# Gate stage of a fused attention and gated-MLP kernel: engine queues in the order of a walked list, row scales prepared a block further ahead, half of w_out decoded beside attention

## The chip, the cores and the metric

One core of one Trainium2 chip. The metric is device time in microseconds of one launch, median of several runs. Engines are named as in the profile: PE (TensorE matmul), PEld (its weight loads), DVE (VectorE), ACT (ScalarE), POOL (GpSimd), SP (SyncE, which issues all DMAs here).

## What is computed

```python
def phi(x):                                   # x: (8, 8, 576, 64), w_phi: (64, 128)
    proj = np.einsum('bhsd,df->bhsf', x, w_phi)
    proj = proj - np.max(np.abs(proj), axis=-1, keepdims=True)
    return np.concatenate([np.exp(proj), np.exp(-proj)], axis=-1)
q_p, k_p = phi(q), phi(k)
kv = np.einsum('bhsf,bhsd->bhfd', k_p, v); z = np.sum(k_p, axis=2)
num = np.einsum('bhsf,bhfd->bhsd', q_p, kv)
den = np.einsum('bhsf,bhf->bhs', q_p, z)[..., None] + 1e-06
x = (num / den).transpose(0, 2, 1, 3).reshape(4608, 512)
xn = x / np.sqrt(np.mean(x * x, axis=-1, keepdims=True) + 1e-06) * rms_g
g, val = xn @ w_gate, xn @ w_val              # (512, 1536) each
out = (g / (1 + np.exp(-g)) * val) @ w_out    # w_out: (1536, 512)
```

w_gate, w_val and w_out come as 64-bit floats, the rest as 32-bit.

## The kernel before

Every float32 product is made of three products of operands split into a high and a low half: ACT casts the high half (`_split`, L60) and DVE or POOL subtracts it to get the low one (L61). The 64-bit weights are first decoded to 32 bits by `_decode` (L41 to L56): two ACT scalings (L48, L49), three DVE bit operations (L50 to L52), two POOL multiplications of half the columns (L54) and a DVE addition (L55). The work runs in four stages, whose matmuls follow each other on PE.

**Attention** (loop at L497): 35 rounds over 32 head pairs. Each round merges four streams by place (`_merge`): transposes and projections of one pair, exponentials and the key-value sums of the pair before, the numerators of the one before that, and the division of the oldest, which writes x to DRAM. In each round one piece of `decode_jobs` (w_gate and w_val, 32 pieces) is decoded, placed by `late()` behind the engines' latest instructions. As blocks of 288 rows of x are done, `fill` (L453) multiplies them by the first three column groups of w_gate and w_val: 6 units of 12 matmuls a block (L467), ACT copies out (L470), and the result goes to DRAM unscaled ("raw columns").

**Drain** (L653): the fill units that are left are issued, and between them, `at_once` pieces each, the preparation of the first six weight sets (`prep_w`) and of block 0 (`prep`).

**Gate stage** (L849): 9 blocks of 512 rows, each with the 9 remaining column groups of the two weight matrices. One unit is one block and one column group; it makes the gate and value columns by a seven-product scheme (`Unit.p`), each product six matmuls (L680) in one of the PSUM banks A, B, E, two of each. PE's order is written by hand, with an issue edge from each product to the one before: 1, 5, 7', 2, 6, 3', 4', where a prime is the unit before. Between products ACT copies A to B (L697) and E to c (L702), makes the Silu of A (L706), copies B to u (L710); DVE adds B to c (L713), E to u (L716), multiplies h by B (L719); `end`, a unit later, makes Silu of u (L722, ACT), h's second half (L723, POOL) and stores h. Which instruction of DVE, ACT and POOL stands where is not written: the framework's scheduler sorts them by its own simulated times.

Beside the products run jobs hung on places in the loop (`job`, four places to a unit): `prep` of the next block (squares L591 and L594, POOL sums L595, two matmuls with ones L609 and L610 for the row sums, square root L611, reciprocals L615, normalisation L619, differences L630 and L633, seven operand splits); `gv_raw`, which scales and multiplies the raw columns (DVE L737, ACT L738, POOL L739); three more weight sets in block 0 (differences L544, splits L547 to L550); in blocks 1 to 6, 24 pieces of w_out decoded (L795) and written to DRAM; and in the last block the six operand sets of w_out, read back (L747, L757). A block's seven operands lie in nine buffers `xo`, so five of the next block's wait for the last unit's products.

**Output stage** (L943): 18 groups of 256 rows of h, loaded in one DMA each (`hload`), seven products with w_out (L959), and the output rows stored.

Of the kernel before, what the change touches and what calls it, by code (L numbers as in the profile page):

```python
# [10 lines left out]
I32 = mybir.dt.int32  # L11
# [29 lines left out]
def _decode(nc, pool, raw, n):  # L41
# [6 lines left out]
    nc.scalar.mul(a, high.bitcast(F32), REBASE)  # L48
    nc.scalar.mul(lf, low.bitcast(U32), 2.0 ** -52)  # L49
    nc.vector.tensor_scalar(p, u, 3, None, ALU.logical_shift_left)  # L50
    nc.vector.scalar_tensor_tensor(p, u, -0x80000000, p, ALU.bitwise_and, ALU.bitwise_or)
    nc.vector.tensor_scalar(u, p, -0x00800000, None, ALU.bitwise_and)  # L52
    for h in (slice(0, n // 2), slice(n // 2, n)):
        nc.gpsimd.tensor_tensor(a[:, h], lf[:, h], a[:, h], ALU.mult)  # L54
    nc.vector.tensor_tensor(a, p.bitcast(F32), a, ALU.add)  # L55
    return a  # L56
# [26 lines left out]
def kernel(ctx: ExitStack, tc: tile.TileContext, q, k, v, w_phi,  # L83
# [20 lines left out]
    XPAD, OPAD, RPAD = 192, 64, 192  # L104

# [53 lines left out]
    ps_f = ctx.enter_context(tc.tile_pool(name="ps_f", bufs=2, space=PSUM))  # L159
# [20 lines left out]
    a_ctx = ExitStack()  # L180
    dec = a_ctx.enter_context(tc.tile_pool(name="a_dec", bufs=1))
    ld = a_ctx.enter_context(tc.tile_pool(name="a_ld", bufs=2))
    wk = a_ctx.enter_context(tc.tile_pool(name="a_wk", bufs=2))
    const = a_ctx.enter_context(tc.tile_pool(name="a_const", bufs=1))
    pad(a_ctx, 192)
    big = a_ctx.enter_context(tc.tile_pool(name="a_big", bufs=2))
# [35 lines left out]
    def decode_jobs():  # L222
        jobs, late_ = [], []
# [16 lines left out]
        for j in range(NJ):  # L240
            for c0 in range(0, DM, CH):
                keep(late_, w_out, wos, j * 128, c0, CH)
        return jobs, late_

    def decode_pieces(jobs, dec):
        raws = {}

        def piece(i):
# [5 lines left out]
            with late():  # L254
                jobs[i][2](_decode(nc, dec, raw, jobs[i][1]))
# [219 lines left out]
    early, decs_late = decode_jobs()  # L475
# [21 lines left out]
    for i in range(PR + 3):  # L497
# [9 lines left out]
        dq += 1  # L507
# [16 lines left out]
        if PR - 2 <= i < PR:  # L524
            raw_gv(i - PR + 2)
    a_ctx.close()


    g_ctx = ExitStack()
# [8 lines left out]
    pg_ctx = ExitStack()  # L538
    ps_g = pool(pg_ctx, "m_ps_g", 2, space=PSUM)
    bank = lambda n: ps_g.tile([128, 512], F32, name=n)  # L540

    def sums7(w, rows):

        sub = lambda o, a, b, op=ALU.subtract: nc.vector.tensor_tensor(w[:, o], w[:, a], w[:, b], op)  # L544
        w_ = w.rearrange("p o c f -> p o (c f)")
        wt = rows.rearrange("p h o c f -> p h o (c f)")
        return sub, [lambda: nc.scalar.copy(wt[:, 0, 0:3], w_[:, 0:3]),  # L547
                     lambda: nc.gpsimd.tensor_tensor(wt[:, 1, 0:3], w_[:, 0:3], wt[:, 0, 0:3].bitcast(F32), ALU.subtract),
                     lambda: nc.scalar.copy(wt[:, 0, 3:7], w_[:, 1:5]),
                     lambda: nc.vector.tensor_tensor(wt[:, 1, 3:7], w_[:, 1:5], wt[:, 0, 3:7].bitcast(F32), ALU.subtract)]  # L550

    W = {}
    ROW = {1: 0, 2: 1, 4: 2, 3: 3, 6: 4, 5: 5, 7: 6}

    def prep_w(j, pl):

        d = {}

        def one_():
            d["w"] = w = raws.pop(j)  # L560
            W[j] = pl.tile([128, 2, 7, 2, 128], F32R, name=f"w{j}")
            d["sub"], d["p"] = sums7(w, W[j])
            d["sub"](4, 0, 3)
            d["sub"](3, 3, 2, ALU.add)
            d["p"][0]()
            d["p"][1]()

        def two():
            d["sub"](2, 3, 0)
            d["sub"](1, 1, 2)  # L570
            d["p"][2]()
            d["p"][3]()
        return [one_, two]

    def fetch(bk):
        x = xm.tile([128, NC, T], F32, name="x")
        nc.sync.dma_start(out=x, in_=xsv[:, :, bk * T:(bk + 1) * T])
        return x

    xb = {}  # L580
    seeds = []

    def prep(bk):

        d = {}
        ops = xb[bk] = {}

        def square(c):
            if c == 0:
                ops["ri"] = xm.tile([128, T], F32, name="ri", bufs=2)  # L590
                nc.scalar.activation(ops["ri"], d["x"][:, 0], AF.Square)  # L591
                return
            sq = xm.tile([128, T], F32, name="t", bufs=2)
            nc.scalar.activation(sq, d["x"][:, c], AF.Square)  # L594
            nc.gpsimd.tensor_tensor(ops["ri"], ops["ri"], sq, ALU.add)  # L595

        def total():
            sh = xm.tile([128, T], F32R, name="t", bufs=2)
            sl = xm.tile([128, T], F32R, name="t", bufs=2)
            _split(nc, sh, sl, ops["ri"], lo_eng=nc.gpsimd)  # L600
            d["s"] = sh, sl

        def scale():
            if not seeds:
                for _ in range(2):
                    seeds.append(bank("B"))
                    nc.tensor.matmul(seeds[-1], ones, d["s"][0], start=True, stop=True)
            sp = fp()
            nc.tensor.matmul(sp, ones, d["s"][0], start=True, stop=False)  # L609
            nc.tensor.matmul(sp, ones, d["s"][1], start=False, stop=True)  # L610
            nc.scalar.activation(ops["ri"], sp, AF.Sqrt, scale=1.0 / DM, bias=eps)  # L611

        def inverse(c):
            ri = ops["ri"][:, c * 256:(c + 1) * 256]
            nc.vector.reciprocal(ri, ri)  # L615

        def normal(c):
            x = d["x"]
            nc.vector.scalar_tensor_tensor(x[:, c], x[:, c], g[:, c:c + 1], ops["ri"], ALU.mult, ALU.mult)  # L619

        part = lambda k, h: d["x"][:, 2 * k:2 * k + 2, h * HT:(h + 1) * HT]

        def split(n, v, lo):
            o = xp.tile([128, 2, 2, HT], F32R, name="xo")
            _split(nc, o[:, 0], o[:, 1], v, lo_eng=lo)
            ops[n] = o

        def third():
            d["t3"] = xm.tile([128, 2, HT], F32, name="t", bufs=2)
            nc.vector.tensor_tensor(d["t3"], part(1, 1), part(0, 1), ALU.subtract)  # L630

        def sub(o, a, b):
            nc.vector.tensor_tensor(part(*o), part(*a), part(*b), ALU.subtract)  # L633

        P, V = nc.gpsimd, nc.vector
        return ([lambda: d.update(x=fetch(bk))]
                + [lambda c=c: square(c) for c in range(NC)] + [total, scale]
                + [lambda c=c: inverse(c) for c in range(2)] + [lambda c=c: normal(c) for c in range(NC)]
                + [third, lambda: split(1, part(0, 0), P), lambda: sub((0, 1), (0, 1), (0, 0)),
                   lambda: split(5, part(0, 1), P)],  # L640
                [lambda: split(2, part(1, 0), P), lambda: sub((0, 0), (1, 1), (0, 1)),
                 lambda: split(6, part(0, 0), P), lambda: sub((1, 0), (1, 0), (0, 0)),
                 lambda: split(7, d["t3"], P), lambda: split(3, part(1, 1), P), lambda: split(4, part(1, 0), P)])

    first, rest = prep(0)
    ahead = []
    for j in range(JL):
        ahead += prep_w(j, wl6) + [lambda j=j: raw_gv(j + 2)]
    pre = first + rest
    ahead = [ahead[0], pre[0]] + [p for ab in zip(ahead[1:], pre[1:]) for p in ab] + pre[len(ahead):]  # L650
    n = 0
    at_once = -(-len(ahead) // RES)
    while units or here or fills:  # L653
        if len(units) <= 6 and here:
            units.extend(fill(*here.pop(0), nc.gpsimd, [fp, lambda: bank("A")]))
        units.pop(0)()
        for _ in range(at_once):
            if ahead:
                ahead.pop(0)()
        load_x()  # L660
    while ahead:
        ahead.pop(0)()
    f_ctx.close()
    pad(ctx, RPAD, side="right")
    wr3 = pool(ctx, "w_r", 1, side="right")
    k_ctx = ExitStack()
    wk = pool(k_ctx, "wk", 2, side="right")

    def product(o, n, x, w, first):
        last = next(i for i in reversed(nc.cur_bb.bb.instructions) if i.engine == mybir.EngineType.PE)  # L670
        with tc.issue_after(last):
            product_(o, n, x, w, first)

    def product_(o, n, x, w, first):
# [10 lines left out]
    class Unit:  # L685
# [3 lines left out]
        def __init__(u, bk, j):  # L689
            u.bk, u.j, u.x, u.w = bk, j, xb[bk], W[j]  # L690

        def p(u, n):
            if n == 1:
                u.A = bank("A")[:, LO]
                product(u.A, 1, u.x, u.w, True)
                u.B = bank("B")[:, LO]
                nc.scalar.copy(u.B, u.A)  # L697
            elif n == 5:
                u.E = bank("E")[:, LO]
                product(u.E, 5, u.x, u.w, True)  # L700
                u.c22 = wk.tile([128, HT], F32, name="c22", bufs=3)
                nc.scalar.copy(u.c22, u.E)  # L702
            elif n == 2:
                product(u.A, 2, u.x, u.w, False)
# [318 lines left out]
```

## Time and profile before

| | us |
|---|---|
| median of 3 runs | 1378.99 |
| runs | 1374.15, 1385.33, 1378.99 |
| profiled execution, its own time | 1373.07 |
| span of that execution, first to last instruction | 1371.3 |
| granted TensorE clock, mean over the span | 0.972 of full speed |

A row of instructions reads: start, time on the engine, engine, source line, operation, tile written <- tiles read, shape, count; in brackets the idle time of that engine just before it and what ended it. A row of a group reads: line, engine, operation, tiles, shape, count, then busy us and mean ns of one, then idle time ahead of it and its causes. A row of a stage reads: from:to and its length, then for PE, PEld, DVE, ACT, POOL the busy us and the count of instructions, then the granted clock (1.00 is full speed), the share of the DMA engines' time in use, and GB/s. Matmuls overlap, so the distance of their starts is their price, not their own time; a few records of matmuls can be missing.

### The profile page before, as it was taken

The numbers are of one execution on the slowest core, as the hardware profiler recorded it, in microseconds if no ns is written. First come the engines' busy times: TensorE is split into PE (matmuls) and PEld (weight loads), VectorE is DVE, ScalarE is ACT, GpSimd is POOL, SyncE is SP. The second block draws the span as 40 slices with busy tenths as digits, with TensorE's granted clock in tenths as the row PEclk, the third lists the DMA queues.
The fourth block names the chain that finished last, engine by engine and source line by source line (L and its number), as shares of the span: only waits on it lengthen the run. The fifth ranks groups of instructions, "written<-read, shape, count | busy, mean of one in ns | idle before, by whom it ended". The sixth has DMA issues, their size and how long they took to land. (4 is left out here: it accounts for less than half of the span.)

```text
span 1371.3 us, 28126 instructions
## 1 busy us (share of the span) xinstructions
PE 1258.1 (92%) x10202; PEld 1233.9 (90%) x10202; DVE 1023.6 (75%) x1451; ACT 809.1 (59%) x1849; POOL 843.2 (61%) x775
## 2 busy tenths in 40 slices
PE   7989999999999986897988988889789889999998
PEld 7989999999999986896988988879789879999998
DVE  6898977888778746618477685776754769999996
ACT  5978876877787754444556555456455533343432
POOL 3665754566565565636556654665545457888885
PEclk9999999999999997999999999999999989999999
DMA  6456666566556336534443443434421443535441
GB/s 162 123 139 165 172 173 191 142 164 186 155 157 187 100 102 189 179 129 153 136 137 132 163 135 109 148 136 140 147 101 70 163 161 116 178 124 169 139 139 47
DMA packets 206698, 197.40 MB, mean 144 GB/s; under 512 B 69792, under 2 KB 173600, under 8 KB 206560
## 3 DMA queue, kind: packets, MB, share of 16 engines
q1 hardware_dynamic: 206560, 195.60, 46.5%
q8 instruction: 81, 1.33, 0.4%
q14 instruction: 57, 0.47, 0.1%
HBM read 126.04 MB, written 69.50 MB: 143 GB/s over the span
## 5 line engine op out<-in xcount | busy, mean ns | idle before, releaser
L373 POOL TENSOR_TENSOR ql<-eq,qh 128x256 fp32r<-128x256 f32 x256 | 216.4, 876 | 75.4 <-issue 51.8
L680 PE MATMUL B<-xo,w 128*128 128x256 f32 x1458 | 215.1, 285 | 5.7 <-DVE c L713 3.9
L680 PEld LDWEIGHTS B<-xo,w 128*128 128x128 f32 x1458 | 193.4, 196 | 7.2 <-DVE c L713 4.9
L680 PE MATMUL A<-xo,w 128*128 128x256 f32 x972 | 147.2, 289 | 36.7 <-ACT B L697 36.4
L680 PEld LDWEIGHTS A<-xo,w 128*128 128x128 f32 x972 | 129.4, 196 | 43.0 <-ACT B L697 42.3
L680 PE MATMUL E<-xo,w 128*128 128x256 f32 x972 | 144.0, 285 | 18.9 <-DVE u L716 18.8
L61 POOL TENSOR_TENSOR xo<-st,xo 128x768 fp32r<-128x768 f32 x54 | 126.8, 2360 | 44.7 <-ACT xo L60 42.9
L680 PEld LDWEIGHTS E<-xo,w 128*128 128x128 f32 x972 | 127.7, 194 | 22.8 <-DVE u L716 22.7
L308 DVE TENSOR_REDUCE mx<-pp 128x4 f32<-128x512 f32 (+1 forms) x160 | 101.0, 632 | 44.9 <-PE pp L306 43.4
L344 PE MATMUL acc<-vm,ek 128*128 128x65 f32 x1024 | 131.0, 267 | 0.7 <-ACT ek L331 0.5
L60 ACT CAST xo<-st 128x768 fp32r<-128x768 f32 x54 | 43.4, 836 | 148.9 <-DVE st L912 70.3
L723 POOL TENSOR_TENSOR h<-u,c 128x256 f32<-128x256 f32 x81 | 70.5, 870 | 96.8 <-ACT u L722 75.1
L344 PEld LDWEIGHTS acc<-vm,ek 128*128 128x128 f32 x1024 | 126.9, 192 | 1.2 <-ACT ek L331 1.2
L61 POOL TENSOR_TENSOR xo<-x,xo 128x512 fp32r<-128x512 f32 (+1 forms) x72 | 106.3, 1488 | 26.1 <-ACT xo L60 25.0
L467 PE MATMUL fp<-xo,fg 128*128 128x288 f32 x576 | 97.3, 308 | 8.1 <-ACT fo L470 6.6
L369 ACT ACTIVATE qh<-sm 128x512 fp32r<-128x512 f32 (+1 forms) x192 | 97.1, 506 | 0.0
L467 PEld LDWEIGHTS fp<-xo,fg 128*128 128x128 f32 x576 | 84.7, 196 | 9.8 <-ACT fo L470 7.7
L304 PE MATMUL pp<-wh,th 128*128 128x256 f32 x288 | 88.2, 307 | 4.6 <-DVE yr L311 3.4
L61 POOL TENSOR_TENSOR xo<-w,xo 128x768 fp32r<-128x768 f32 x36 | 91.6, 2543 | 0.0
L368 ACT ACTIVATE eq<-sm 128x512 f32<-128x512 f32 x128 | 78.3, 611 | 17.3 <-PE sm L357 16.5
L959 PE MATMUL gy<-w,xo 128*128 128x256 f32 x648 | 79.5, 281 | 6.2 <-ACT xo L60 5.6
L959 PEld LDWEIGHTS gy<-w,xo 128*128 128x128 f32 x648 | 76.9, 192 | 7.1 <-ACT xo L60 6.0
(164 smaller groups left out, 3439.3 us busy)
## 6 DMA issues: line engine op xcount, KB each, us to landing
w<-hs SPq DMA_DIRECT2D x18, 1536.0 KB
hs<-h SPq DMA_DIRECT2D x81, 256.0 KB
gvs<-fo SPq DMA_DIRECT2D x96, 144.0 KB
gvr<-gvs SPq DMA_DIRECT2D x54, 256.0 KB
rc<-di SPq DMA_DIRECT2D x32, 288.0 KB
x<-xs SPq DMA_DIRECT2D x16, 576.0 KB
x<-xs SPq DMA_DIRECT2D x9, 1024.0 KB
kt<-in_k_dram SPq DMA_DIRECT2D x32, 256.0 KB
```

The source lines that it names most:

```text
L60: (hi_copy or nc.scalar.copy)(hi, x)
L61: (lo_eng or nc.vector).tensor_tensor(lo, x, hi.bitcast(F32), ALU.subtract)
L304: nc.tensor.matmul(o, th[:, cs], wh, start=True, stop=False)
L308: nc.vector.tensor_reduce(mx[:, 0:2 * m], pp[:, 0:2 * m], axis=AX.X, op=ALU.max, apply_absolute_value=True)
L344: nc.tensor.matmul(acc[:, sg, h], e[h][:, sg, j], vm[:, h, j], start=False, stop=(h == 1 and j == T0 - 1))
L368: nc.scalar.activation(ei[:, sg], yi, AF.Exp, scale=1.0 - 2.0 * sg)
L369: nc.scalar.activation(hi[:, sg], yi, AF.Exp, scale=1.0 - 2.0 * sg)
L373: nc.gpsimd.tensor_tensor(lo[:, sg, cs], ei[:, sg, cs], hi[:, sg, cs].bitcast(F32), ALU.subtract)
L467: nc.tensor.matmul(fp[:, 0:TF], w, xx[x][:, c], start=(i == 0), stop=(i == 3 * NC - 1))
L680: nc.tensor.matmul(o, a, e, start=(first and i == 0), stop=(i == 5), skip_group_check=True)
L723: nc.gpsimd.tensor_tensor(u.h[:, HI], u.u2, u.c22, ALU.mult)
L959: nc.tensor.matmul(place[n], a[:, kp], w[:, o], start=(first and kp == 0 and i == 0), stop=(kp == KP - 1 and i == 2), skip_group_check=True)
```

## The change

- From the end of attention to the end of the gate stage, every instruction of DVE, ACT, POOL and PE gets an issue edge from the one before it on its engine (`InOrder`), so that each engine's queue is the order in which the program writes them. SP's DMAs get none.
- That order is made by `Flow`: a list of tasks with an engine (or two to choose from: PV, VP), a modelled duration, and what they depend on. The products are written one after the other; each advances a modelled time (0.685 us, 1.6 for a fill unit), its evictions are put at once on their engines (`core`), and then `step` writes those tasks of the list, by priority, whose inputs are modelled done and whose engine is free or will have finished within 1.2 us (1.9 in the drain). A task that a product needs and that is not yet written is written then (`need`). Loads are modelled at 5 to 7 us. The square root, 3 us with its tables, may go only behind product 1.
- The order of products is 1, 5, 7', 3', 2, 6, 4', the Silu of the second half follows product 6, u is kept in h's second half. B has three banks, A and E two, S one (row sums, and the difference for operand 5, which now goes to PSUM); the two fill banks end with the drain's first units, and later fill units use A and E.
- Row scales (`scales`) are a task set of their own, for the block after next, from four separate 256 KB loads of x; reciprocals are four of 128 columns for two of 256. `prep` loads x again.
- w_out: pieces 0 to 11 are decoded beside attention (1.6 pieces a round in rounds 12 to 31), with their last addition on POOL; 12 to 17 in the drain, in buffers of `xo`; the last six in blocks 1 to 6.
- Attention's pools are in another order in memory, constants and results lowest, decode buffers highest.

The diff's core:

```diff
-        dq += 1
+        dq += 1 + (ATT / 20 if 12 <= i < 32 else 0)
...
+                jobs[i][2](_decode(nc, dec, raw, jobs[i][1], nc.gpsimd if i >= 2 * NC + 24 else nc.vector))
...
+            def call(*a, **k):
+                with ExitStack() as es:
+                    if self.last is not None:
+                        es.enter_context(tc.issue_after(self.last))
+                    r = f(*a, **k)
+                self.last = next(i for i in reversed(tc.nc.cur_bb.bb.instructions) if i.engine == self.kind)
+                return r
...
+        def need(self, *ts):
+            for t in ts:
+                if t["done"] is None:
+                    self.run(t)
+                self.now = max(self.now, t["done"] + self.HOP)
...
+            if t["big"]:
+                return r <= self.now and self.free[e] <= self.now + 0.6 and self.roomy
+            return r <= (self.now if e in "QT" else max(self.now, self.free[e])) and (
+                e in "QT" or self.free[e] <= self.now + 0.05
+                or max(r, self.free[e]) + (t["dur"] if not isinstance(t["dur"], dict) else t["dur"][e]) <= self.now + self.room)
...
+            q.append(add("Q", 5.0, lambda c=c: chunk(c), a[c - 2] if c > 2 else scale_t[0], behind=q[-1:]))
+            s.append(add("S", 0.62, lambda c=c: square(c), q[c]))
+            a.append(add("P", 1.35, lambda c=c: total(c), s[0], s[c], a[c - 1]))
...
+        sc = add("T", 0.5, scale, l, after=("banks",), ring=ring["S"], frees=frees)
+        r = add("S", 3.0, root, sc, big=True)
+        inv = [add("V", 0.87, lambda c=c: inverse(c), r) for c in range(4)]
...
+        VP = dict(V=1.0, P=1.45)
+        f = add("Q", 7.0, fetch, *used[0])
+        nm = [add("V", 0.9, lambda c=c: normal(c), f, *inv) for c in range(NC)]
...
+            ld = ring["r"] = flow.add("Q", 6.0, load, behind=[ring["r"]], ring=ring["gvr"], frees=frees)
+            s = flow.add("V", 0.9, scaled, ld, *xt[bk]["ri"])
+            s = flow.add("S", 0.42, silu, s)
+            s = flow.add("PV", dict(P=0.95, V=0.5), mul, s)
...
     for bk in range(NB):
+        raw_block(bk)
         if bk + 1 < NB:
+            prep(bk + 1, JN - 1)
+        if bk + 2 < NB:
+            scales(bk + 2)
...
+        for j in order:
+            u = Unit(bk, j)
+            for who, n in ((u, 1), (u, 5), (old, 7), (old, 3), (u, 2), (u, 6), (old, 4)):
+                if who is None:
+                    continue
+                who.p(n)
+                if n == 6 and old:
+                    old.silu()
+                flow.roomy = n == 1
+                flow.step(1.2)
+            old = u
```

More of the change, by code (lines that the diff above doesn't have):

```diff
@@ L575, in fetch @@
[L575 to L586, printed above, removed]
-        def square(c):
[L589 to L601, printed above, removed]
+    BANKS = dict(A=2, B=3, E=2, S=1)
@@ L603, in scale @@
         def scale():
             if not seeds:
-                for _ in range(2):
+                for _ in range(BANKS["B"]):
                     seeds.append(bank("B"))
[L607 to L611, printed above, removed]
+                    nc.tensor.matmul(seeds[-1], ones, d["sh"], start=True, stop=True)
@@ L635, in prep @@
[L635 to L667, printed above, removed]
+        add = flow.add
+        q = [add("Q", 5.0, lambda: chunk(0), *scaled_t.get(bk - 3, ()))]
+        s = [add("S", 0.62, lambda: square(0), q[0])]
+        a = [None]
+        for c in range(1, NC):
+            q.append(add("Q", 5.0, lambda c=c: chunk(c), a[c - 2] if c > 2 else scale_t[0], behind=q[-1:]))
+            s.append(add("S", 0.62, lambda c=c: square(c), q[c]))
+            a.append(add("P", 1.35, lambda c=c: total(c), s[0], s[c], a[c - 1]))
@@ L669, in product @@
     def product(o, n, x, w, first):
[L670 to L674, printed above, removed]
         i = 0
@@ new lines, in fill_unit @@
+    def fill_unit(m, bk, j, wi, n):
+        d = xs_t[m]
+        flow.need(*d["t"])
+        js = slice(j * 128, (j + 1) * 128)
+        o = bank("AE"[n % 2])[:, 0:TF]
+        i = 0
+        for c in range(NC):
+            a, al = wf1[wi][:, 0, c, js], wf1[wi][:, 1, c, js]
+            for w, h in ((a, 0), (a, 1), (al, 0)):
+                nc.tensor.matmul(o, w, d["o"][:, h, c], start=(i == 0), stop=(i == 3 * NC - 1))
+                i += 1
+        flow.mark(("unit", n), 1.6)
+        f = fxp.tile([128, TF], F32, name="fo", bufs=6)
+        flow.core("S", 0.42, lambda: nc.scalar.copy(f, o))
+        nc.sync.dma_start(out=gvv[j][:, wi, bk * TF:(bk + 1) * TF], in_=f)
@@ new lines @@
+    flow.pri = -2
+    for m, (bk, x) in enumerate(blocks_left[:2]):
+        fill_tasks(m, bk, x)
+    flow.pri = -1
+    make_w(0, lambda: wl6, True)
+    scales(0)
+    for k in range(min(ATT, npieces), NDEC0):
+        decode_out(k, True)
+    prep(0)
+    make_w(1, lambda: wl6, True)
+    for j in range(2, JN):
+        flow.pri = -1 if j < JL else 0
+        make_w(j, lambda j=j: wl6 if j < JL else wr3, False, () if j < JL else ("right",))
+    flow.pri = 1
+    scales(1)
+    n = 0
+    while units:
+        units.pop(0)()
+        flow.mark(("unit", n), 1.6)
+        n += 1
+        if len(units) % (2 * J1) == 0:
+            flow.marks.add(("fill", len(units) // (2 * J1) and -2 or -1))
+        flow.step(1.9)
@@ new lines @@
+    pf_ctx.close()
+    pg_ctx = ExitStack()
+    ps_g = pool(pg_ctx, "m_ps_g", 1, space=PSUM)
+    flow.marks.add("banks")
+    for m, (bk, _) in enumerate(blocks_left):
+        for jj in range(2 * J1):
+            fill_unit(m, bk, *divmod(jj, 2), n)
+            n += 1
+            if jj == 0 and m + 2 < len(blocks_left):
+                flow.pri = -2
+                fill_tasks(m + 2, *blocks_left[m + 2])
+            if jj == 2 * J1 - 1:
+                flow.marks.add(("fill", m))
+            flow.step(1.9)
@@ L812 @@
+    f_ctx.close()
+    pad(ctx, RPAD, side="right")
+    wr3 = pool(ctx, "w_r", 1, side="right")
+    flow.marks.add("right")
+    k_ctx = ExitStack()
+    wk = pool(k_ctx, "wk", 2, side="right")
+    done = NDEC0
+    old = None
     for bk in range(NB):
-        for n in range(2 * J1):
-            job(bk, (n + 1) * NS, lambda bk=bk, n=n: gv_raw(bk, n))
-            job(bk, (n - 1) * NS, lambda bk=bk, n=n: load_r(bk, n))
+        order = LAST if bk == NB - 1 else range(JN)
+        flow.pri = 10 * bk + 3
+        raw_block(bk)
+        flow.pri = 10 * bk + 2
@@ L873 @@
-    older.end()
+            prep(bk + 1, JN - 1)
+        if bk + 2 < NB:
+            scales(bk + 2)
+        flow.pri = 10 * bk + 4
+        while done < NDEC0 + (npieces - NDEC0) * min(bk, NB - 3) // (NB - 3):
+            decode_out(done)
+            done += 1
+        if bk == NB - 1:
+            for kp in range(KP):
+                make_o(kp)
+            flow.add("Q", 7.0, lambda: hload(0), after=tuple((bk, LAST[HSLOT[0]], n) for n in ROW))
+        for j in order:
[9 more added lines that the diff above has]
+            old = u
```

538 lines of the change are left out of this document (347 added, 191 removed).

## The prediction, made before any run of the changed kernel

> **What bounds the kernel now.** I read the page first, then a table of busy time cut at the stages' ends, then who waited for whom on PE in the gate stage, then single instructions around one boundary of blocks.
>
> ```profile
> PE 1258.1 (92%) x10202; PEld 1233.9 (90%) x10202; DVE 1023.6 (75%) x1451; ACT 809.1 (59%) x1849; POOL 843.2 (61%) x775
> ```
>
> PE is the busiest engine, so the question is where it isn't working at full speed. By stage (us from:to, length, then busy us and count of PE, PEld, DVE, ACT, POOL, then granted clock and DMA share):
>
> ```profile
> 0.00:497.00 497.00, 474.54 (x3866) 466.12 (x3867) 400.67 (x712) 388.09 (x964) 289.59 (x372) 1.00 0.56 155
> 497.00:610.70 113.70, 95.70 (x653) 93.28 (x653) 50.76 (x45) 50.70 (x102) 58.34 (x38) 0.91 0.51 162
> 610.70:1097.80 487.10, 425.83 (x3420) 413.92 (x3418) 324.78 (x513) 269.51 (x641) 278.50 (x276) 0.96 0.40 134
> 1097.80:1122.90 25.10, 18.60 (x127) 17.68 (x128) 17.42 (x14) 7.29 (x11) 11.74 (x6) 0.80 0.46 151
> 1122.90:1371.30 248.40, 243.38 (x2144) 242.88 (x2142) 229.96 (x168) 93.49 (x134) 205.04 (x85) 0.99 0.40 132
> ```
>
> They are attention, the drain of the remaining fill units, the gate stage, the start of the output stage, and the output stage. What the middle two would take without loss comes from undisturbed neighbours, a fill unit of 12 matmuls and a gate product of 6:
>
> ```profile
> 588.30 1.76 PE L467 MATMUL fp<-xo,fg 128*128 128x288 f32 x12
> 589.90 1.76 PE L467 MATMUL A<-xo,fv 128*128 128x288 f32 x12
> ...
> 663.38 0.84 PE L680 MATMUL B<-xo,w 128*128 128x256 f32 x6
> 664.06 0.84 PE L680 MATMUL A<-xo,w 128*128 128x256 f32 x6
> ...
> 497.00:611.00 114.00, 94.04 (x646) 92.25 (x646) 0.91 0.52 162
> ```
>
> A unit starts every 1.60 us, a product every 0.68 us. The last row counts the fill matmuls of the drain: 646/12, or 54 units, 86.4 us; with the scale products about 88, so the drain of 113.7 loses 25.7. The gate stage has 9 blocks x 9 units x 7 products = 567, x 0.68 = 385.6, with some 3.5 us of scale products 389; it takes 487.1 and **loses 98**. The output stage runs at its pace. So some 124 us can be won, 98 of them in the stage that the change rewrites. What PE waited for there (us in total, times, longest):
>
> ```profile
> PE A L680 <- ACT B L697: 36.4, 25, 3.3
> PE E L680 <- DVE u L716: 18.8, 14, 3.3
> PE B L680 <- DVE c L713: 3.9, 4, 1.7
> ```
>
> That is 59 of the 98. One boundary shows how, and what the other 39 are:
>
> ```profile
> 743.92 0.98 PE L680 MATMUL A<-xo,w 128*128 128x256 f32 x6 [0.79 <-ACT B L697]
> ...
> 748.93 0.97 PE L680 MATMUL E<-xo,w 128*128 128x256 f32 x6 [1.20 <-DVE u L716]
> ...
> 753.53 1.24 PE L680 MATMUL A<-xo,w 128*128 128x256 f32 x6 [2.92 <-ACT B L697]
> 754.56 1.48 PE L680 MATMUL B<-xo,w 128*128 128x256 f32 x6
> 755.84 1.48 PE L680 MATMUL E<-xo,w 128*128 128x256 f32 x6
> ```
> ```profile
> 739.88 1.28 ACT L611 ACT_TABLE_LOAD   x1
> 741.18 0.69 ACT L611 ACTIVATE ri<-fp,eps 128x512 f32<-128x512 f32 x1
> 741.88 1.28 ACT L722 ACT_TABLE_LOAD   x1
> ...
> 752.79 0.42 ACT L738 ACTIVATE gvr<-gvr 128x256 f32<-128x256 f32 x1 [2.47 <-DVE gvr L737]
> 753.12 0.36 ACT L697 COPY B<-A 128x256 f32<-128x256 f32 x1
> ```
> ```profile
> 741.90 3.36 DVE L615 RECIPROCAL ri<-ri 128x256 f32<-128x256 f32 x2 [0.43 <-ACT ri L611]
> ```
>
> The first wait is the square root with its two table loads, 3.3 us on ACT just ahead of the copy A to B that PE's next product needs. The second follows from 3.4 us of reciprocals on DVE. The third is the worst: ACT stands 2.47 us at a Silu of the raw columns whose scaling is late on DVE, and the 0.36 us copy, long ready, is queued behind it. After 2.92 us without work PE's products start 1.28 us apart (754.56 to 755.84), not 0.68; that, and shorter refills, is the rest of the 98. So the loss is not lack of an engine: DVE is busy 325 of 487. It is small urgent instructions standing behind others in their engine's queue.
>
> The Trainium skill (TensorE: Matmul & The Clock Gate, Part 1) gives about 3.4 us of idleness before the clock halves. By that rule no wait here would slow the clock, since the longest is 3.3, and only the 59 could be won; the trace shows halving after 2.92, and decides.
>
> **The change part by part.** *Written order* (issue edges on DVE, ACT, POOL, PE): no instruction is added, cost nothing in itself. What it does is choose the queue positions. Around each product the list admits work only when its inputs are modelled done and it ends within 1.2 us, or the engine is free; the square root only behind product 1's copy. The mechanism of all three waits above is aimed at.
>
> *Product order* 1,5,7',3',2,6,4' (primes: the unit before) for 1,5,7',2,6,3',4': between product 1 and product 2, which waits for the A copy, now stand three products (2.04 us) for two (1.36); between 3' and the next use of its E bank four (2.72) for two. Against it, from 6 to the 7 that needs ACT's copy of B three for four. The two slacks that grow belong to 55 of the 59 us. The third B bank and the single scale bank come from the two fill banks; with it ACT's copy no longer waits for the multiplication two units back.
>
> *Decoding w_out*: 24 pieces in the gate stage become 6; 12 go beside attention, 6 to the drain. A piece costs, by these rows (last figures: busy us, mean ns):
>
> ```profile
> L50 DVE TENSOR_SCALAR wc<-wc 128x256 int32<-128x256 int32 x24 | 15.8, 660 | 1.2 <-ACT wc L48 1.2
> L51 DVE SCALAR_TENSOR_TENSOR wc<-wc 128x256 int32<-128x256 int32 x24 | 17.0, 710 | 0.4
> L52 DVE TENSOR_SCALAR wc<-wc 128x256 int32<-128x256 int32 x24 | 12.8, 535 | 0.6
> L55 DVE TENSOR_TENSOR wc<-wc 128x256 f32<-128x256 f32 x24 | 15.8, 658 | 8.7 <-POOL wc L54 8.7
> L54 POOL TENSOR_TENSOR wc<-wc 128x128 f32<-128x128 f32 x48 | 26.3, 570 | 22.5 <-DVE wc L52 16.1 <-ACT c L702 6.4
> L48 ACT ACTIVATE wc<-wc 128x256 f32<-128x256 f32 x24 | 10.5, 437 | 0.0
> L49 ACT ACTIVATE wc<-wc 128x256 f32<-128x256 uint32 x24 | 10.4, 433 | 0.0
> ```
>
> DVE 2.56, POOL 1.14, ACT 0.87 us; 18 of them take 46 us off DVE, 20 off POOL, 16 off ACT in the gate stage, and 2 DMAs each off SP. Beside attention 12 pieces x 1.9 us on DVE (their last add goes to POOL) are 23 us over 20 of its 35 rounds, some 20/35 x 497 = 284 us. How much room is there:
>
> ```profile
> 100.00:250.00 150.00, 146.10 (x1208) 143.20 (x1207) 126.10 (x228) 118.75 (x297) 85.88 (x109) 1.00 0.62 168
> ...
> 350.00:400.00 50.00, 50.00 (x419) 49.97 (x418) 39.27 (x69) 38.60 (x99) 26.71 (x33) 1.00 0.54 159
> ```
>
> Late in attention DVE is 79% busy and PE never idle; with the pieces it is at 87%, close to 100 to 250 (84%), where PE idles 2.6%. So between 0 and 0.026 x 284 = 7 us; I take **+4**, the middle, since the stretch it is nearest to has fewer fill products to cover PE.
>
> *Scales two blocks ahead*: the same squares, sums and root, off the boundary, reciprocals in four of 128 columns for two of 256. It reads x a second time, 4 loads of 256 KB a block into buffers that POOL's sum frees; a load that waits for one holds SP's queue, with h stores and raw loads behind it, and three h buffers cover about two units, 9.5 us. Without that cover ACT's Silu would wait for h. Added bytes (7 blocks x 1 MB) and removed ones (18 pieces x 0.38 MB) about cancel; the DMA share of 0.40 over 487 us becomes near 0.48. I cost it at 0. The difference for operand 5 now goes to PSUM and its low half to DVE: 8 blocks x about 1 us more there.
>
> *What the gate stage keeps.* DVE 325-46+8 = 287, POOL 258, ACT 254 of about 410: at most 70%. No engine binds on the mean. Bounds on the loss: 0 (the list is perfect) and 98 (nothing won). I take 21, nearest the quiet rows, because pieces stay tight. The boundary above loses 0.79+1.20+2.92, and 1.8 in three slow products, 6.7 in all; I leave a fifth of that, 1.3, at each of eight boundaries, where five operands can only be split as the last unit frees their buffers, about 10; and not quite one boundary's worth in block 0, which prepares three weight sets (6), and in the last, which prepares six (5). Gate 389+21 = 410, **-77**.
>
> *Drain*: 9.2 of its waits is one event, ACT standing at the first square until x lands, with the fill's copies behind it:
>
> ```profile
> 517.02 0.37 SPq L577 DMA_DIRECT2D x<-xs  x1
> ...
> 525.85 0.63 ACT L591 ACTIVATE ri<-x 128x512 f32<-128x512 f32 x1 [7.48 <-DMA x<-xs]
> ...
> 528.16 3.25 PE L467 MATMUL A<-xo,fv 128*128 128x288 f32 x12 [9.18 <-ACT fo L470]
> ```
>
> By the order of the pools that x lay in the memory of attention's last results; the moved pools put it into that of attention's work and decode buffers, free earlier. In the new drain the fill units also come first and the square's load is listed ahead of its use. DVE gets 15, POOL 7 us of decode more in the drain, and block 1's scales, on 51 and 58 of 114 busy. Bounds 0 and 25.7 won; I take six lost, **-20**. The start of the output stage (25.1 for 14.3) keeps its chain, the output split behind the last h: 0, bounds -8 and +4.
>
> Sum, against the profiled execution's 1373.1: +4-77-20 = 1280. The three runs' median, 1379.0, lies 5.9 above that execution, so for a median **1286**.
>
> **Rivals.** *A, DVE and POOL stretch each other* (0.22). In the 690 to 800 stretch (ns min/median/max):
>
> ```profile
> L61 POOL TENSOR_TENSOR xo<-x,xo x12: 1287/1314/1810, 697.2 to 776.0; 128x512 fp32r<-128x512 f32 x12
> L619 DVE SCALAR_TENSOR_TENSOR x<-x,g,ri x10: 739/982/1767, 694.6 to 799.4; 128x512 f32<-128x512 f32 x10
> ```
>
> The list plans 0.9 for this DVE operation. Squeezed into 410 us the two engines meet more often; 13 operations of its size a block (4 normalisations, 3 differences, 6 scalings) at the worst, 1.77 for 0.9, are 11 us on DVE's 287/9 = 32 of a block's 43: full. Then half the loss stays, 49 for 21: 1286+28 = 1314. For it speaks the spread, against it the undisturbed 0.68 us pace of the rows at 663, with DVE and POOL at work then too. The Trainium skill (SBUF — State Buffer, SBUF: two separate sides) calls this an exclusive lock on a shared port pair, which speaks against a list that plans both engines as free; the row agrees so far that 739 plus the rest of one POOL operation of 1314 can make 1767.
>
> *B, the list is nearly right* (0.08): gate 394, drain 90: 1286-20 = 1266.
>
> *C, slower* (0.07): a fixed order stands where a load is late. The list allots 5 to 7 us; x took 8.8 from issue in the drain. Beyond 5.0 that is 3.8, less 2.04 of slack 1.8, and half of the 1.8 that three slow products cost makes 2.7 us of PE per late load. A block has some 12 loads (4 of chunks, 1 of x, 6 of raw columns, 1 of w_out), 100 in all. It decides from 34 late ones on, (1379-1286)/2.7; half of them late give 1286+135 = 1421. Against it:
>
> ```profile
> L737 DVE TENSOR_TENSOR gvr<-gvr,ri 128x512 f32<-128x512 f32 x54 | 48.2, 910 | 4.1 <-DMA gvr<-gvs 3.7 <-issue 0.3
> ```
>
> 54 raw loads cost DVE 3.7 us now.
>
> *D, the order isn't what it says* (0.06): the issue edges bind only the order of writing; if the modelled clock drifts, fillers again stand ahead, and only the decoding that left counts: 18 of 24 pieces, a share of 46/325 of the loss, 14 us: 1379-14+4 = 1369.
>
> **How the numbers follow.** Forecast 0.57, with its own range 1264 to 1306. Range 1250 to 1345: it takes in B, also with the output stage's start 8 and attention 4 better (1254), A, and A with the drain unwon (1334), and leaves out C and D, 0.13. A measurement here tells about 1% from no change; faster 0.57+0.22+0.08 = 0.87, same 0.06, slower 0.07.
>
> **What would show it.** Right: a gate stage near 410, the waits for L697's copy and L716's sum falling from 55 to under 15 us, no ACT or DVE wait ahead of a product above 2 us, a drain near 94, 0 to 2% PE idleness late in attention. Wrong: POOL and DVE means growing with the gate near 440 (A), ACT or DVE waiting for DMA in the gate stage (C), or boundaries still losing the 6.7 us of the one above (D).

## The result and the profile after

The changed kernel takes **1291.56 us** (1283.46 to 1295.45, 4 runs) beside 1378.07 (1374.15 to 1385.33, 4 runs): a ratio of 0.936, 95% interval 0.930 to 0.942. The profiled execution took 1292.9, with a span of 1291.1. Its line of busy times:

```profile
PE 1234.7 (96%) x10203; PEld 1218.8 (94%) x10203; DVE 1017.1 (79%) x1503; ACT 807.5 (63%) x1849; POOL 788.3 (61%) x741
```

By stage, cut within 0.4 us at the same events as before (us from:to, length, busy us and count of PE, PEld, DVE, ACT, POOL, granted clock, DMA share, GB/s):

```profile
0.00:506.60 506.60, 478.19 (x3866) 467.13 (x3866) 415.13 (x745) 396.89 (x988) 307.06 (x407) 0.99 0.58 162
506.60:604.00 97.40, 90.72 (x654) 89.18 (x654) 71.57 (x83) 54.68 (x115) 56.77 (x44) 0.98 0.77 238
604.00:1002.90 398.90, 392.07 (x3418) 390.23 (x3416) 295.62 (x487) 244.85 (x599) 208.24 (x197) 1.00 0.51 163
1002.90:1030.00 27.10, 17.45 (x96) 16.19 (x95) 24.82 (x20) 12.64 (x18) 19.40 (x9) 0.69 0.54 178
1030.00:1291.10 261.10, 256.31 (x2177) 256.10 (x2175) 210.00 (x169) 98.48 (x132) 196.79 (x86) 1.00 0.37 122
```

Attention grew from 497.0 to 506.6 (+9.6), the drain went from 113.7 to 97.4 (-16.3), the gate stage from 487.1 to 398.9 (**-88.2**), and from the last gate product to the end it is 288.2 for 273.5 (+14.7). Their sum, -80.2, is the difference of the two spans. In the gate stage PE hardly waits any more (us in total, times, longest; the list's helper records every operation at one line, L549):

```profile
PE B L549 <- DVE c L549: 3.5, 2, 2.2
PE E L549 <- ACT w L549: 1.8, 1, 1.8
PE E L549 <- DVE w L549: 0.8, 1, 0.8
PE B L549 <- ACT h L549: 0.5, 1, 0.5
PE E L549 <- DVE h L549: 0.2, 1, 0.2
```

6.8 us for 59. The waits have turned round: now ACT and DVE stand idle until PE has finished, which is what a stage bound by PE looks like. The views of ACT's and of DVE's own waits in that stretch:

```profile
ACT h L549 <- PE A L549: 65.0, 62, 1.7
...
ACT h L549 <- DMA hs<-h: 8.1, 4, 2.8
```
```profile
DVE h L549 <- PE B L549: 43.5, 45, 2.0
DVE c L549 <- PE B L549: 37.2, 37, 2.0
```

**Two paces.** The output stage does the same products in both kernels, yet they start further apart. First the kernel after, then the same kernel in another execution:

```profile
1110.19 4.40 PE L1203 MATMUL gy<-w,xo 128*128 128x256 f32 x36
1114.43 4.40 PE L1203 MATMUL gz<-w,xo 128*128 128x256 f32 x36
```
```profile
1107.38 4.24 PE L1203 MATMUL gy<-w,xo 128*128 128x256 f32 x36
1111.46 4.24 PE L1203 MATMUL gz<-w,xo 128*128 128x256 f32 x36
```

36 products take 4.24 us (117.8 ns each) in the one and 4.08 (113.3) in the other, at a granted clock of 1.00 in both. The profile of before has 4.08. That is 4.5 of 117.8, or 3.8% of every stretch that runs at the slow pace, and it has to be taken out before stages are compared.

### The profile page after: what moved, and what is told of

Same layout as the page of the kernel before. It is cut to its first block, busy times and chain, and to the rows that moved or that the text cites. A ratio compares the mean times of both kernels' runs of the same rounds, so it can differ in the third digit from the quotient of the medians.

```text
span 1291.1 us, 28132 instructions
## 1 busy us (share of the span) xinstructions
PE 1234.7 (96%) x10203; PEld 1218.8 (94%) x10203; DVE 1017.1 (79%) x1503; ACT 807.5 (63%) x1849; POOL 788.3 (61%) x741
## 4 chain that ended last, share of the span: by engine, by line
PE 50%; DVE 2%; issue 1%; DMA 1%; ACT 1%; POOL 0%; DVEq 0%; POOLq 0%; ACTq 0%
PE B L549 12%; PE E L549 9%; PE A L549 9%; PE gd L1203 6%; PE gy L1203 6%; PE gz L1203 6%; PE fp L1203 3%; DMA hs<-h 1%; DVE wc L549 1%; DVE xo L61 0%; PE S L549 0%; DVE gvr L549 0%; DVE w L1154 0%; ACT L549 0%; DVE w L549 0%
## 5 line engine op out<-in xcount | busy, mean ns | idle before, releaser
L549 PE MATMUL B<-xo,w 128*128 128x256 f32 x1458 | 193.4, 277 | 4.0 <-DVE c L549 3.5
L549 PEld LDWEIGHTS B<-xo,w 128*128 128x128 f32 x1458 | 178.9, 188 | 5.2 <-DVE c L549 3.9
L549 POOL TENSOR_TENSOR h<-h,c 128x256 f32<-128x256 f32 x81 | 62.8, 775 | 149.1 <-ACT h L549 125.2
L549 PE MATMUL E<-xo,w 128*128 128x256 f32 x972 | 137.4, 277 | 2.8 <-ACT w L549 1.8
L549 PE MATMUL A<-xo,w 128*128 128x256 f32 x972 | 137.0, 277 | 0.0
L549 PEld LDWEIGHTS E<-xo,w 128*128 128x128 f32 x972 | 122.7, 188 | 3.4 <-ACT w L549 2.0
L549 PEld LDWEIGHTS A<-xo,w 128*128 128x128 f32 x972 | 122.7, 188 | 0.0
L54 POOL TENSOR_TENSOR wa<-raw,wa 128x192 f32<-128x192 f32 (+1 forms) x88 | 53.9, 633 | 76.1 <-DVE wa L52 25.7
L60 ACT CAST xo<-w 128x768 fp32r<-128x768 f32 x72 | 59.0, 833 | 62.4 <-PE gd L1203 24.2
L373 ACT ACTIVATE eq<-sm 128x512 f32<-128x512 f32 x128 | 78.0, 609 | 16.3 <-PE sm L362 14.7
L311 PE MATMUL pp<-wh,tl 128*128 128x256 f32 x288 | 83.0, 298 | 1.5 <-DVE tl L61 1.5
L310 PE MATMUL pp<-wl,th 128*128 128x256 f32 x288 | 81.2, 283 | 0.0
```

The costliest lines, as they stand in the source:

```text
L60: (hi_copy or nc.scalar.copy)(hi, x)
L310: nc.tensor.matmul(o, th[:, cs], wl, start=False, stop=False)
L311: nc.tensor.matmul(o, tl[:, cs], wh, start=False, stop=True)
L373: nc.scalar.activation(ei[:, sg], yi, AF.Exp, scale=1.0 - 2.0 * sg)
L549: r = f(*a, **k)
```

## The experiments

All are single profiles for the stages, medians for the times. "Slow" is how many us of gate and output stage ran at the slow pace (runs of at least six products into one bank whose starts lie 117 to 118.5 ns apart in the mean, summed); "span less pace" is the span minus 3.8% of that. "Out" reaches from the last gate product to the end. Ratios are to the kernel before in runs beside it.

| kernel | median us | ratio (95%) | attention | drain | gate | out | slow | span less pace |
|---|---|---|---|---|---|---|---|---|
| before | 1378.07 | 1 | 497.0 | 113.7 | 487.1 | 273.5 | 78 | 1368.4 |
| after | 1291.56 | 0.936 (0.930 to 0.942) | 506.6 | 97.4 | 399.0 | 288.1 | 295 | 1279.9 |
| after, again | 1285.14 | 0.935 (0.929 to 0.940) | 508.0 | 99.0 | 397.6 | 277.1 | 1 | 1281.6 |
| no edges | 1388.52 | 1.006 (1.002 to 1.010) | 511.0 | 111.7 | 488.1 | 267.2 | 57 | 1375.8 |
| edges alone | 1419.35 | 1.032 (1.027 to 1.038) | 498.1 | 116.8 | 526.2 | 280.0 | 317 | 1409.0 |
| scales one ahead | 1386.01 | 1.004 (1.001 to 1.007) | 506.4 | 95.2 | 507.9 | 278.0 | 178 | 1380.6 |
| old product order | 1299.25 | 0.940 (0.934 to 0.946) | 507.2 | 98.7 | 408.0 | 289.4 | 320 | 1291.2 |
| no early pieces | 1285.22 | 0.928 (0.922 to 0.935) | 500.3 | 98.0 | 409.8 | 277.0 | 179 | 1278.3 |
| six early pieces | 1283.39 | 0.928 (0.921 to 0.936) | 500.2 | 100.8 | 402.4 | 278.7 | 61 | 1279.8 |
| pieces alone | 1385.78 | 1.007 (1.002 to 1.011) | 511.3 | 112.0 | 483.4 | 283.0 | 334 | 1377.0 |
| last sum on DVE | 1294.89 | 0.937 (0.930 to 0.944) | 506.9 | 100.1 | 399.8 | 286.8 | 257 | 1283.9 |
| sets first | 1287.46 | 0.934 (0.928 to 0.941) | 503.8 | 99.4 | 402.3 | 287.7 | 316 | 1281.2 |

**No edges.** The walked list still writes the code, but DVE, ACT and POOL need not keep to it:

```diff
-            self.vector, self.scalar = InOrder(tc.nc.vector, E.DVE), InOrder(tc.nc.scalar, E.Activation)
-            self.gpsimd, self.tensor = InOrder(tc.nc.gpsimd, E.Pool), InOrder(tc.nc.tensor, E.PE)
+            self.vector, self.scalar = tc.nc.vector, tc.nc.scalar
+            self.gpsimd, self.tensor = tc.nc.gpsimd, InOrder(tc.nc.tensor, E.PE)
```

> The changed kernel without the issue edges on DVE, ACT and POOL; the walked list, banks, product order and PE's order stay, the framework's scheduler sorts the three queues again. Theory (the written queue order removed the waits): waits for the A copy and the E addition come back at the boundaries, gate stage 440 to 480 us instead of 399, total 1335 to 1375. Rival 1 (product order with its longer slacks, the third B bank and the 18 pieces that left did it): gate stage stays 395 to 415, total 1285 to 1310.

The gate stage is back at 488.1, above my range of 440 to 480, and PE's waits there are back too, in other places:

```profile
PE B L549 <- DVE c L867: 49.1, 28, 7.1
PE B L549 <- ACT h L874: 8.1, 5, 3.4
PE A L549 <- ACT B L862: 8.0, 7, 3.1
```

Everything else of the change is in this kernel (scales ahead, product order, 18 fewer pieces in the gate stage), and it gains nothing there. Of the rivals on record for the prediction, D would have had the edges bind nothing; they carry the gain.

**Edges alone.** The reverse: the kernel before with the same edges on all four engines in its own written order, no list.

```diff
+    nc = Engines()
...
+    nc = tc.nc
```

> The kernel before, with the same in-order edges on all four engines in its gate stage, but following the order in which its code was already written: no walked list, scales one block ahead, all of w_out decoded in the gate stage. My theory: what the change gains in the gate stage needs both, the list's order and the queues that keep to it; edges alone in the old order leave the gate stage at 487 us or above, time 1375 to 1430 (waits of the products can grow, because nothing may step around a late instruction any more). Rival 1: any fixed order of the queues brings most of it: gate stage 440 us or less, time about 1330. Rival 2: the scheduler's choice was no worse than the written order and the edges change nothing: within 1% of 1378.

The gate stage takes 526.2, about 522 without its 101 us at the slow pace. Fixed in the order in which its code was already written, the stage does worse than with the scheduler's choice: new waits appear at the scales of the next block (18.4 for t), ahead of which nothing may now be taken.

```profile
PE E L539 <- DVE u L539: 35.8, 25, 3.2
PE B L539 <- DVE c L539: 25.4, 16, 3.6
PE fp L539 <- ACT t L539: 18.4, 8, 2.6
```

**Scales one ahead.** The list stays, the scales lose their block of distance:

```diff
-    scales(1)
...
+            scales(bk + 1)
             prep(bk + 1, JN - 1)
-        if bk + 2 < NB:
-            scales(bk + 2)
```

> The changed kernel with row scales prepared for the next block only, as before, instead of the one after. Theory: the square root and the reciprocals have a place of their own in the list, so the extra block is only distance; gate stage 399 to 407. Rival (the distance is needed: the chain of loads, squares, sums, root, reciprocals, normalisation and splits does not fit one block without holding PE): 2 to 5 us a block, gate stage 415 to 440, total 1308 to 1333.

My theory fell: the gate stage went to 507.9, 21 us above that of before (17 without the slow pace in both). (One of its ten runs took 6935 us, unexplained; the others 1383 to 1395.) One boundary in that kernel, on ACT, on DVE and on PE:

```profile
747.69 0.69 ACT L549 ACTIVATE ri<-S,eps 128x512 f32<-128x512 f32 x1
...
760.04 0.61 ACT L549 CAST xo<-x 128x512 fp32r<-128x512 f32 x1
```
```profile
750.60 1.76 DVE L549 RECIPROCAL ri<-ri 128x128 f32<-128x128 f32 x2
...
755.55 1.00 DVE L549 SCALAR_TENSOR_TENSOR x<-x,g,ri 128x512 f32<-128x512 f32 x1
```
```profile
760.69 0.39 PE L549 MATMUL A<-xo,w 128*128 128x256 f32 x1 [0.58 <-ACT xo L549]
762.66 0.85 PE L549 MATMUL A<-xo,w 128*128 128x256 f32 x5 [1.59 <-POOL xo L549]
764.47 0.41 PE L549 MATMUL E<-xo,w 128*128 128x256 f32 x1 [0.95 <-ACT xo L549]
```

The chain root (747.7), reciprocals (750.6), normalisation (755.6), first split (760.0) is 13 us long and ends as the next block's first product is due; the remaining operands then come one by one, and PE starts and stops through them. Over the stage PE waits 51 us for the operands `xo`, and 293 products start 208 to 218 ns after the one ahead, at about half pace. At all eight boundaries the root starts 12.5 to 13.0 us before the block's first product.

In the second execution of the changed kernel the chain takes as long, but stands earlier. Root and first split of one block, on ACT:

```profile
747.50 0.69 ACT L549 ACTIVATE ri<-S,eps 128x512 f32<-128x512 f32 x1
...
761.12 0.62 ACT L549 CAST xo<-x 128x512 fp32r<-128x512 f32 x1
```

This root is the fifth of nine and belongs to the next block, whose first product comes only at 783.50, 36 us later; for the other blocks it is about 50 us or more. At that boundary PE runs through, one product each 0.68 us:

```profile
782.14 1.52 PE L549 MATMUL B<-xo,w 128*128 128x256 f32 x12
783.50 0.84 PE L549 MATMUL A<-xo,w 128*128 128x256 f32 x6
784.18 0.84 PE L549 MATMUL E<-xo,w 128*128 128x256 f32 x6
```

**Old product order.** The loop over products goes back to 1,5,7',2,6,3',4', with the silu's step behind 3'.

> The changed kernel with the products in the order of before, 1, 5, 7', 2, 6, 3', 4', and the Silu of the second half directly behind 3'. Theory: the written order gives most, the product order a minor part; slack for the A copy falls from 2.04 to 1.36 us and for the E bank from 2.72 to 1.36, so single waits of up to 0.7 us come back, 10 to 25 us in the gate stage (409 to 424), total 1300 to 1315. Rival 1 (the slacks did it): 35 us or more come back, total above 1325. Rival 2 (slack is worth nothing once queues are in order): gate stage within 4 us of 399.

408.0, or 405.5 without its 64 us at the slow pace, beside 397.6: the order is worth 8 us of the gate stage, just under what I expected.

**No early pieces, six early pieces.** `ATT = 0` and `ATT = 6` in place of 12.

> The changed kernel with no piece of w_out decoded beside attention: 6 in the drain, 18 in blocks 1 to 6, three a block. Theory: attention goes back from 506.6 to about 497 us (the pieces cost it 9.6), and the gate stage hides the 12 pieces, DVE there at 295+31 of 400, so it grows by 0 to 5 us; total 1283 to 1290 against 1292. Rival (the lighter gate stage is what lets the list run without waits): gate stage 415 or more, total 1300 or more. A third: attention stays at 504 or more, because its pools were moved in memory, not because of the pieces.

> The changed kernel with six pieces of w_out beside attention in place of twelve; twelve are left to the gate stage beside the six of the drain. Theory, halfway between the version without pieces there (attention 500.3, gate stage 409.8) and the changed kernel (506.6, 398.9): attention about 503.5, gate stage about 404, so the sum stays within 2 us, and with the pace of the output stage taken out the time does too. Rival: the gate stage has room for six more without loss (its waits are 7 us in all and stand in its first 60 us), so it stays within 2 us of 399 and the sum gets 3 us shorter.

Attention ends 6.3 us earlier with none, at 500.3 where I expected 497, and as early with six (500.2). With none the gate stage is 10.8 us longer; without the slow pace it takes 403.0 beside 397.6, so about 5 us of that are work. Beside the two medians of the changed kernel, these versions' lie 0 to 8 us lower, but their spans less pace (1278.3 and 1279.8) are within 4 us of those of the changed kernel (1279.9, 1281.6). So the number of pieces moves time from one stage to the other and gains nothing that these runs show.

**Pieces alone.** The kernel before with twelve pieces beside attention.

> The kernel before with one part of the change alone: twelve of the 24 pieces of w_out decoded beside attention, the rest as it was. My theory: without the list a product's wait in the gate stage is one of order and not of load, so the freed 12 pieces bring little there (0 to 10 us off 487), while attention pays about 6 us (497 to 503): time within 1% of 1378. Rival: the gate stage of before is bound by the load of DVE and ACT, and shrinks in proportion, by 25 us or more: time about 1355.

Ratio 1.007: the theory, with a dearer attention (511.3, about 14 more) than expected. The gate stage lost only 4 us with 12 pieces fewer, so before the change it was not bound by load. PE's largest wait there has hardly moved, 31.9 for 36.4:

```profile
PE A L680 <- ACT B L697: 31.9, 25, 3.0
```

**Last sum on DVE.** In `_decode`'s call, `nc.vector` for all pieces.

> The changed kernel with one part undone: the last sum of the twelve early pieces of w_out goes back from POOL to DVE (the pieces stay beside attention). Theory, from the piece-alone kernel whose attention ended at 511 with the sum on DVE against 504 to 508 with it on POOL: DVE is the engine that is late there, so attention ends 2 to 5 us later than 506.6 (508 to 512), the rest is unchanged; time 1288 to 1297. Rival: the attention stage is late because of the pieces' loads and casts, wherever the sum stands: attention within 1.5 us of 506.6, time within 0.3% of the changed kernel's.

Attention 506.9, within the rival's bound: where the sum stands doesn't matter there. The time (1284.07 to 1295.43 in three runs, 1307.36 in the fourth) is too scattered to tell 3 us.

**Sets first.** `flow.pri = 10 * bk + (3 if bk < NB - 1 else 5)` for the raw loads' step.

> The changed kernel, with one number changed: in the last block the raw loads' step is put behind the making of w_out's six operand sets, so that these stand ahead in the walked list. My theory of the start of the output stage (three of six operand sets are made only after the last product and cost about 5 us more than before): the stretch from the last gate product to the end gets 3 to 8 us shorter, the gate stage stays within 4 us of 399, and no wait of a product for a w of w_out stands after the last gate product. Rival: the sets are late because ACT and POOL have no room for them in the last block at all; the same work is only moved, and the gate stage grows by what the output stage gains: time within 0.4% of 1291.

Nothing came earlier. The stretch to the end lost 0.4 us, and the cast of the first late set, 11.7 us behind the last gate product's end in the changed kernel (1014.63 against 1002.9), is at 1017.13 against 1005.5 here. The number changed no place that matters, so this run doesn't say what earlier sets would bring. They pass two at a time through the two `wc` buffers; a third one wasn't tried.

**After, again**, for the two paces:

> The changed kernel once more, unchanged, for the two paces of the output stage (36 products in 4.08 us in the kernel before and in two of the experiments, in 4.24 us in the changed kernel and in one). Theory: the pace is picked at the last restart of TensorE by chance, so that one build shows either in different executions: single times of this build then differ by about 10 us, and this execution may show 4.08. Rival: the pace belongs to the build (its instructions and their places): 4.24 again, with single times within 4 us of each other apart from the known scatter.

The same kernel, the other pace: 4.08 throughout, and the stretch to the end is 11.0 us shorter (277.1 for 288.1). So the pace of the output stage belongs to the execution and not to the build.

**Stops.** The first cast of two groups of rows is done 37 times:

```diff
+            for _ in range(36 if n == "a11" and gi_ in (2, 5) else 0):
+                nc.scalar.copy(h, x)
```

> The changed kernel with work added to make TensorE stop: in the output stage the first cast of two groups of rows (the third and the sixth) is done 37 times instead of once, which holds ScalarE about 30 us and TensorE for some of it. Theory: the pace of the products (36 in 4.08 or in 4.24 us) is picked anew when TensorE restarts after a stop, so the stretches between the stops (each at full granted clock) show both paces, or the one before a stop differs from the one behind it in at least one place. Rival: the pace is set once in an execution, and all three stretches have the same one.

PE stood 21.5 and 23.1 us, and all three stretches ran at 4.08: a stop of that kind does not by itself switch the pace. (Time 1346.04, one run.) But its gate stage ran slow from 649 to 1009 and so took 412.1, with the instructions of the changed kernel. Twelve products in this kernel, then in the changed kernel's second execution:

```profile
706.05 1.58 PE L549 MATMUL B<-xo,w 128*128 128x256 f32 x12
707.46 0.87 PE L549 MATMUL A<-xo,w 128*128 128x256 f32 x6
```
```profile
705.05 1.52 PE L549 MATMUL B<-xo,w 128*128 128x256 f32 x12
706.41 0.84 PE L549 MATMUL A<-xo,w 128*128 128x256 f32 x6
```

1.41 against 1.36 us. So the pace can change within an execution, and what changed it here stays open.

## Why the prediction was right, and where not

The forecast was 1286 with its own range 1264 to 1306; measured 1291.56 and, in a second set of runs, 1285.14. The sum was right because errors cancelled. Term by term, on the profiled span, predicted and measured: attention +4 and +9.6, drain -20 and -16.3, gate -77 and -88.2, out 0 and +14.7; together -93 and -80.2. The 5.9 that the forecast added for a median was scatter of one execution: the two medians of the changed kernel lie 1.3 below and 1.7 above their profiled executions.

**The waits.** "The mechanism of all three waits above is aimed at": shown. L697's copy and L716's sum, 55 us before, cost PE less than 1 us (of the six waits that are left four stand in block 0 and two at the last products), and the kernel without edges shows that the queues' order does it. With the waits the half pace went: before, 157 products of the gate stage start 208 to 218 ns after the one ahead, about 100 ns late, 16 of the 98 us; after, none does. One sign did not come: ACT waited three times 2.2 to 2.8 us for h's stores and DVE once 5.6 us for ACT, but no product waited for that.

**The gate's floor and loss.** The floor of 389 held: 397.6 at the fast pace. Of the 21 us of loss, block 0 was nearly right (46.6 us in the second execution for 60 products, 5.3 over their pace, for the 6 allowed), the end was somewhat dear (3.5 us, of them 2.7 in two waits, for 5), and the eight boundaries were wrong: from its first product to that of the next, each of blocks 1 to 6 takes 43.3 us, which is 63 x 0.68 and 0.46 for its two scale products, and block 7, without these, 42.8. I had left 1.3 us at each boundary; they lose nothing. That is most of the 11 us.

**"I cost it at 0"**, of the scales two blocks ahead, is the step that failed, though the sum doesn't show it. Without them the same list makes a gate stage of 507.9. The quoted rows had the start of the reason: root, reciprocals, normalisation and first split are a chain, 13 us long, and it must end before the block's first product. I looked at what the move adds to queues and not at what its absence would keep on the path. One block of distance need not be too little: in the kernel before, from block 2 on, the root stood 31 to 35 us before that product. A list that keeps one block and starts the chain earlier in it was not tried. The gain is no sum of parts: edges without list, list without edges, and list without distance each gain nothing, all three together 88. The third B bank and the single scale bank, which every kernel with the list has, were not tested apart.

**Attention** was mis-sized: +9.6 (+11.0 in the second execution) for bounds 0 to 7. I put all of it down to PE idleness like that of 100 to 250, over 284 us. Two windows of before, of after and without early pieces (second column length, then PE):

```profile
160.00:240.00 80.00, 77.27 (x630) 75.39 (x630) 62.89 (x115) 60.84 (x150) 41.16 (x54) 1.00 0.65 181
280.00:360.00 80.00, 79.91 (x664) 79.60 (x664) 65.64 (x111) 60.84 (x153) 44.66 (x56) 1.00 0.61 169
```
```profile
160.00:240.00 80.00, 74.83 (x597) 73.20 (x596) 65.42 (x118) 61.45 (x151) 43.38 (x55) 0.98 0.62 173
280.00:360.00 80.00, 77.45 (x634) 76.27 (x633) 67.15 (x117) 62.29 (x154) 47.17 (x59) 1.00 0.65 184
```
```profile
160.00:240.00 80.00, 75.74 (x617) 73.81 (x616) 62.97 (x114) 60.54 (x150) 41.37 (x54) 1.00 0.64 172
280.00:360.00 80.00, 79.94 (x664) 79.64 (x662) 65.04 (x110) 60.92 (x153) 46.82 (x57) 1.00 0.62 172
```

63 matmuls fewer in these 160 us, at 0.12 us some 8 us late. In 280 to 360 the loss of 30 is the pieces' alone; in 160 to 240, 13 of the 33 remain without them. Most of these 13 are within scatter: the kernel with edges alone, whose attention is that of before, has 621 there. Whether the memory pools that moved cost the rest isn't shown.

**Drain**: six us of loss were left, and there are 9 to 11. The square's wait of 9.18 us is gone; the largest that remain are three short ones.

```profile
PE E L549 <- ACT fo L549: 5.0, 3, 2.0
```

**Out: 0, with bounds of -8 to +4.** Of the +14.7, 11.0 is the pace, which no reading of the trace of before could have sized, although it has both paces; the second execution has +3.6, inside the bounds. There PE stands for the splits of w_out's and of h's operands and then runs at half pace, 13 products in 2.94 us, double the fast pace's 1.47:

```profile
1011.31 3.14 PE L1203 MATMUL fp<-w,xo 128*128 128x256 f32 x13 [2.94 <-DVE xo L61]
1014.25 2.59 PE L1203 MATMUL gy<-w,xo 128*128 128x256 f32 x13
```

**The rivals.** A (DVE and POOL stretch each other) did not come: the normalisations of 690 to 800 take 987 ns in the mean for 1090 before, with the two engines squeezed into less time (1054 for 1131 over the whole stage). Not every operation stayed as short: POOL's sums of squares take 1569 for 1292 in the mean over the stage, and no product waited for them.

```profile
L619 DVE SCALAR_TENSOR_TENSOR x<-x,g,ri 128x512 f32<-128x512 f32 x10 | 10.5, 1090 | 0.0
```
```profile
L549 DVE SCALAR_TENSOR_TENSOR x<-x,g,ri 128x512 f32<-128x512 f32 x12 | 11.5, 987 | 0.0
```

C (late loads) would show ACT or DVE waiting for a load; ACT's only waits for DMA (8.1 us, four times) are for h's stores to free their buffers, and they cost PE nothing. D fell with the kernel without edges. B's gate stage of 394 came nearest.

## What to carry to other kernels

When small urgent instructions stand behind others in an engine's queue, an order walked with modelled times and enforced on every engine can win nearly all of it back, as here, where it needed its long chain to start well ahead of the product that waits for it; test the parts one by one, since here none of the three was worth anything alone. Cost a move by the chain that it takes off the path, not only by the instructions that it adds. Before two profiles are compared stage by stage, compare the start distance of equal products, and run the same build twice.

## What the hardware showed beyond that

Products of 256 columns start 113.3 or 117.8 ns apart, both at a granted clock of 1.00, for stretches of some 2 to over 400 us, and one build shows either. In thirteen profiles the slow share of gate and output stage ran from 1 us (the second execution) to 374 (the one with stops). In the kernel before, the switch has a regular place. In its blocks 1 to 7 the two scale products of 512 columns stand alone among the others, with 18 products between them, and each of these 14 changes the pace of those behind it, from fast to slow or back:

```profile
847.88 0.39 PE L609 MATMUL fp<-t,ones 128*128 128x512 f32 x1
848.11 0.87 PE L680 MATMUL A<-xo,w 128*128 128x256 f32 x6
848.82 0.87 PE L680 MATMUL B<-xo,w 128*128 128x256 f32 x6
...
850.23 0.39 PE L610 MATMUL fp<-t,ones 128*128 128x512 f32 x1
850.46 0.85 PE L680 MATMUL B<-xo,w 128*128 128x256 f32 x6
851.14 0.84 PE L680 MATMUL A<-xo,w 128*128 128x256 f32 x6
```

Six products take 0.71 us between the two and 0.68 behind the second. In the kernel with the pieces alone 12 of 14 do so. In the kernels with list and edges the two scale products stand side by side, and 7 of 64 such pairs changed the pace. Of a sample of eleven switches in seven of the profiles, four stand at such a pair, five at a wait of 0.2 to 1.9 us, and two at a delay of 0.1 to 0.2 us with no wait shown. Not every such place switches the pace, nor did two stops of over 20 us, and why a lone product of 512 columns should do it stays open. The Trainium skill (TensorE: Matmul & The Clock Gate, Part 1, Wait — 56ns, not 53.3ns?) gives columns over 2.4 GHz plus about 2.5 ns for back-to-back warm matmuls, an estimate of 109.2 ns here; the trace, in which every matmul has a weight load of its own (10203 of each), has neither that nor one figure only.
